# The thirteenth row of w_down in a staircase of small loads, ahead of the other twelve

## The chip, the cores and the metric

The kernel runs on one core of a Trainium2 chip. The metric is the device time of one execution in microseconds, as the median of several runs; lower is better. All engines of the core (TensorE, VectorE, ScalarE, GpSimd, SyncE) run their own instruction streams and meet at semaphores. Loads are issued by SyncE (SP in the profile) and carried out by the core's 16 DMA engines.

## The reference

One token goes through a decode step: attention over a cache of 4096 positions with 32 heads, then a gated feed-forward block, each behind a layer norm and with a residual.

```python
q = (x @ wq).reshape(B, Sq, Hq, Dh).transpose(0, 2, 1, 3)          # 640 -> 32 x 128
scores = jnp.einsum("bhqd,bhkd->bhqk", q, k) * (Dh ** -0.5)        # k_cache: 1 x 32 x 4096 x 128
o = jnp.einsum("bhqk,bhkd->bhqd", softmax(scores), v)
attn = o.transpose(0, 2, 1, 3).reshape(B, Sq, Hq * Dh) @ wo        # 4096 -> 640

g = jnp.einsum("bsd,df->bsf", x, w_gate)                           # 640 -> 1728
u = jnp.einsum("bsd,df->bsf", x, w_up)
ffn = jnp.einsum("bsf,fd->bsd", gelu(g) * u, w_down)               # 1728 -> 640

h = x + attn(layernorm(x), k_cache, v_cache, wq, wo)
out = h + ffn(layernorm(h), w_gate, w_up, w_down)
```

All tensors are bf16. The two caches are 32 MB each; with the weights 84 MB are read.

## The kernel before

The 32 heads are done in four groups of eight. For each group the K cache (8 MB) and the V cache (8 MB) are loaded as one transfer each into three large buffers `big`. VectorE multiplies K by the query (`mult`, L338), TensorE folds the products with an identity matrix (`fold`, L302 and L352), VectorE sums them to scores (`red`, L359), `soft` makes the exponentials (L388, L391), and `values` multiplies them with V on TensorE (L404). `Sched` keeps one list of instructions for each engine, in program order; a DMA increments its own semaphore by 16 when it has landed, and a waiting instruction names the count that it needs.

The order of the loads is the program order of SP's list. Behind the last V load come, in this order: `wo` (L445, it waits for the last fold), `w_gate` (L449), `w_up` (L449, it waits for `vfree[2]`, the end of the third group's `values`, since it lies in the buffer which that frees), and then `w_down` in `wd_sb`, which lies behind `w_up` in the same buffer.

`w_down` has 1728 rows of 640 elements. The first 1664 are laid out as 13 consecutive rows for each of the 128 partitions (`NM = 13`), so `wd_sb[:, b, :]` is the row b of every partition; the remaining 64 rows are a fourteenth column (`wd_sb[:, NM, :]`, on partitions 32 to 95), whose other partitions GpSimd fills with zeros first (L454). The loads are called wde (the 64 rows, L455) and wd0, wd1, wd2 (L460): the 13 rows are cut at `WD_CUTS = (0, 9, 12, 13)`, so these three carry 9, 3 and 1 rows for each of 128 partitions, in pieces of 11,520, 3,840 and 1,280 contiguous bytes.

The end of the kernel is a serial path: the output projection (L484), the second layer norm (L267 to L280), the two projections to 1728 (`up`, L502: first `w_gate`, then `w_up`), the transposes of their results to columns (L515), the gelu and the product `hm` (L522 to L531), the product with `w_down` (L537), two copies (L542, L543), one more (L545), and the store of 640 elements (L546). In L537 each of the 14 columns of `hm` is a stationary operand of four matmuls of 160 columns, one for each quarter of the output, on four strips of the array; a group waits for `hm` and for the load that holds its rows. The order of the groups is 13 first, then 0 to 12.

Of the kernel before, what the change touches and what calls it, by code (L numbers as in the profile page):

```python
# [35 lines left out]
NM = 13  # L36
NF = NM + 1
MF = NM * 128
E0 = 32
EP = DF - MF  # L40
WD_CUTS = (0, 9, 12, 13)
QF = NM * 32
NQ = D // 4

# [66 lines left out]
def bass_sequential_preLN__gqa_block_cached__glu_gated_geglu__decode_kernel(  # L111
# [12 lines left out]
    S = Sched(nc)  # L124
# [4 lines left out]
    def at(name, base, off, shape, dt=BF16):  # L129
        return nc.alloc_sbuf_tensor_at(name, shape, dt, offset=nc.lookup_mloc(base).addr + off)  # L130
# [6 lines left out]
    wd_sb = at("wd_sb", big[0], 2 * NC_D * DF, [128, NF, D])  # L137
# [70 lines left out]
    def vec(fn, waits=()):  # L208
        return S.op("vector", fn, waits)
# [33 lines left out]
    kfree, vfree = [None] * NG, [None] * NG  # L243
# [204 lines left out]
    def load_w(name, dst, src, lo, hi, wait):  # L448
# [5 lines left out]
    t_zr = S.op("gpsimd", lambda g: g.memset(wd_sb[:, NM, :], 0.0), [vfree[2]])  # L454
    d_we = S.dma("sync", "wde", lambda s: s.dma_start(  # L455
        wd_sb[E0:E0 + EP, NM, :], B_w_down[MF:DF, :]), [t_zr])
    d_wd = []
    for i in range(len(WD_CUTS) - 1):
        lo, hi = WD_CUTS[i], WD_CUTS[i + 1]
        tok = S.dma("sync", "wd%d" % i, lambda s, lo=lo, hi=hi: s.dma_start(  # L460
            wd_sb[:, lo:hi, :],
            B_w_down[0:MF, :].rearrange("(p b) n -> p b n", b=NM)[:, lo:hi, :]), [vfree[2]])
        d_wd += [tok] * (hi - lo)
    d_wd += [d_we]

    t_clear = vec(lambda v: v.memset(pf[1][:, :].rearrange("p (u x) -> p u x", u=2)[:, :, 0:32 * NF].rearrange(
# [13 lines left out]
    b = None  # L480
    for c in range(QD):
        for j in range(4):
            last = c == QD - 1 and j == 3
            b = S.op("tensor", lambda t, c=c, j=j: t.matmul(  # L484
                pd[32 * j:32 * j + 1, 0:NQ], aP[:, c:c + 1], wo_sb[:, c, j * NQ:(j + 1) * NQ],
                start=False, stop=False, skip_group_check=True), [t_aP, d_wo], token=last)
# [43 lines left out]
    t_u = columns(tu, pu, t_u)  # L530
    t_hm = vec(lambda v: v.tensor_mul(hm[:, :], gu[:, :], u_t), [a, t_u])  # L531

    order = [NM] + list(range(NM))
    for i, s in enumerate(order):
        for j in range(4):
            last = i == len(order) - 1
            b = S.op("tensor", lambda t, s=s, j=j, last=last: t.matmul(  # L537
                pd[32 * j:32 * j + 1, 0:NQ], hm[:, s:s + 1], wd_sb[:, s, j * NQ:(j + 1) * NQ],
                start=False, stop=last, skip_group_check=True),
                [t_hm, d_wd[s]], token=(last and j == 3))  # L540

    t_a = S.op("scalar", lambda a: a.copy(o_sb[:, 2 * NQ:3 * NQ], pd[64:128, 0:NQ]), [b])  # L542
    t_v = vec(lambda v: v.tensor_copy(o_sb[:, 0:NQ], pd[0:64, 0:NQ]), [b])  # L543
# [35 lines left out]
```

## Time and profile before

| | |
|---|---|
| median of 3 runs | 202.84 us (202.81 to 202.94) |
| the profiled execution | 202.74 us, span of the profile 201.5 us |
| TensorE clock granted, mean | 0.82 |
| busy: TensorE, VectorE, ScalarE, GpSimd | 114.3, 120.1, 10.0, 3.5 us |
| DMA | 84.32 MB in 2250 packets, mean 419 GB/s |
| wo, w_gate, w_up: issue to landing | 19.9, 24.6, 26.4 us |
| wd0, wd1, wd2, wde: issue to landing | 28.8, 29.3, 28.0, 26.0 us |

The profile is one execution; its span runs from the first to the last instruction, and 1.2 us of the measured time lie around it. In its lines, SPq is SyncE issuing a DMA, PE a matmul, PEld a weight load of TensorE, and the number behind L is the line of the kernel. A time in brackets is how long the engine sat idle before the instruction and what ended that. The three numbers of a piece of the chain are its start, its length and what it was.

### The profile page before, as it was taken

What the parts mean: (1) busy time and instruction counts of PE and PEld (TensorE: products, weight loads), DVE (VectorE), ACT (ScalarE), POOL (GpSimd) and SP (SyncE); (2) the same over time, 40 slices, a digit from 0 to 9 for tenths busy, and PEclk for the clock granted to TensorE, in tenths of its full rate; (3) what the DMA queues carried; (4) which work ended last, traced back from release to release, by engine and by line L of the source; (5) the groups of instructions that cost most, each with busy time, mean ns of one, the idle gap of its engine ahead of it and who ended that gap; (6) DMA issues with size and microseconds to landing.
All of it is one profiled execution on the core that took longest, in us unless ns stands there. A gap on an engine that the chain in (4) does not pass through costs nothing.

```text
span 201.5 us, 1615 instructions
## 1 busy us (share of the span) xinstructions
PE 114.3 (57%) x850; PEld 24.5 (12%) x560; DVE 120.1 (60%) x91; ACT 10.0 (5%) x28; POOL 3.5 (2%) x21
## 2 busy tenths in 40 slices
PE   1007930098508276876367059966634995864384
PEld 1000100000000030020022000200000033334332
DVE  2000570999993659998440499999899755010232
ACT  3000010000010101000101000000100002010000
POOL 5000000000000000000000000000000001000000
PEclk9999995569966969999967658999996698585855
DMA  7999999999999999999999999999999999999992
GB/s 252 398 586 416 416 429 416 416 416 416 416 416 507 468 468 407 416 429 416 416 418 433 416 416 481 468 455 416 416 442 416 416 429 444 390 407 429 422 403 95
DMA packets 2250, 84.32 MB, mean 419 GB/s; under 512 B 258, under 2 KB 452, under 8 KB 580
## 3 DMA queue, kind: packets, MB, share of 16 engines
q1 hardware_dynamic: 2242, 84.23, 97.2%
q8 instruction: 5, 0.08, 0.2%
q14 instruction: 1, 0.01, 0.0%
q10 hardware_dynamic: 2, 0.00, 0.0%
HBM read 84.23 MB, written 0.00 MB: 418 GB/s over the span
## 4 chain that ended last, share of the span: by engine, by line
DMA 48%; DVE 34%; PE 14%; issue 2%; ACT 1%; SPq 0%; DVEq 0%
DMA big<-in_A_k_cache_dram 35%; DVE big L338 22%; DMA wu_sb<-in_B_w_up_dram 13%; PE pf L302 7%; DVE sc L359 5%; PE pv L404 4%; DVE P L391 2%; DVE xz L328 2%; DVE qm L324 1%; PE pf L502 1%; PE pf L537 1%; PE pf L352 1%; ACT ex L388 1%; DVE mx L381 0%; DVE tu L515 0%
## 5 line engine op out<-in xcount | busy, mean ns | idle before, releaser
L338 DVE TENSOR_TENSOR big<-big,qb 128x8192 bf16<-128x8192 bf16 x16 | 70.2, 4418 | 19.6 <-DMA big<-in_A_k_cache_dram 19.6
L302 PE MATMUL pf<-big,Ibf 128*128 128x512 bf16 x240 | 62.0, 417 | 0.0
L352 PE MATMUL pf<-big,Ibf 128*128 128x512 bf16 x16 | 6.9, 433 | 47.8 <-DVE big L338 24.3
L359 DVE TENSOR_REDUCE sc<-pf 128x64 f32<-128x1024 f32 x16 | 19.3, 1218 | 10.2 <-PE pf L302 10.2
L404 PE MATMUL pv<-big,P 128*32 128x512 bf16 x192 | 15.0, 482 | 3.2 <-DVE P L391 3.2
L352 PEld LDWEIGHTS pf<-big,Ibf 128*128 128x128 bf16 x16 | 1.6, 98 | 94.7 <-DVE sc L359 54.4
L324 DVE TENSOR_TENSOR qm<-pf,hmask 128x1024 f32<-128x1024 f32 x2 | 2.4, 1224 | 17.2 <-PE pf L302 17.2
L316 PE MATMUL pf<-wq_sb,xb 128*128 128x512 bf16 x5 | 2.5, 504 | 12.6 <-DMA wq_sb<-in_A_wq_dram 12.6
L391 DVE TENSOR_TENSOR P<-ex,hmask_bf 128x2048 bf16<-128x2048 bf16 x3 | 6.9, 2293 | 2.0 <-ACT ex L388 2.0
L328 DVE TENSOR_REDUCE xz<-qm 128x128 f32<-128x1024 f32 x4 | 7.5, 1880 | 0.1
L404 PE MATMUL pv<-big,Pl 128*32 128x512 bf16 x64 | 6.1, 560 | 2.4 <-DMA big<-in_A_v_cache_dram 2.4
L404 PEld LDWEIGHTS pv<-big,P 128*32 128x32 bf16 x192 | 5.8, 118 | 11.1 <-issue 5.1
L388 ACT ACTIVATE ex<-sc,nb 128x256 bf16<-128x256 f32 x4 | 2.0, 508 | 86.3 <-DVE mj L385 86.3
L443 DVE TENSOR_TENSOR aT<-pm,rz 128x32 bf16<-128x32 f32 x1 | 0.2, 192 | 9.8 <-PE pm L415 9.8
L484 PE MATMUL pf<-wo_sb,aP 128*1 128x160 bf16 x128 | 3.9, 312 | 3.1 <-DMA wo_sb<-in_A_wo_dram 3.1
L302 PE MATMUL pf<-wq_sb,xb 128*128 128x512 bf16 x15 | 5.4, 480 | 0.0
L399 PE MATMUL pm<-rsm,ones 128*128 128x8 f32 x8 | 1.4, 251 | 6.8 <-ACT rsm L395 6.8
L415 PEld LDWEIGHTS pm<-cred,xm 128*128 128x128 f32 x32 | 4.0, 191 | 8.9 <-issue 6.5
L487 DVE STREAM_TRANSPOSE th<-pf 128x160 f32<-128x160 f32 x1 | 0.3, 350 | 7.6 <-PE pf L484 7.6
L415 PE MATMUL pm<-cred,xm 128*128 128x8 f32 x32 | 4.0, 252 | 1.4 <-ACT xm L412 1.4
L484 PEld LDWEIGHTS pf<-wo_sb,aP 128*1 128x1 bf16 x128 | 3.7, 116 | 3.3 <-issue 3.3
L331 ACT CAST qb<-xz 128x128 bf16<-128x128 f32 x4 | 1.2, 298 | 54.9 <-DVE xz L328 54.9
(85 smaller groups left out, 54.1 us busy)
## 6 DMA issues: line engine op xcount, KB each, us to landing
wq_sb<-in_A_wq_dram SPq DMA_DIRECT2D x1, 5120.0 KB, 15.2
wo_sb<-in_A_wo_dram SPq DMA_DIRECT2D x1, 5120.0 KB, 19.9
wg_sb<-in_B_w_gate_dram SPq DMA_DIRECT2D x1, 2160.0 KB, 24.6
wu_sb<-in_B_w_up_dram SPq DMA_DIRECT2D x1, 2160.0 KB, 26.4
wd_sb<-in_B_w_down_dram SPq DMA_DIRECT2D x1, 1440.0 KB, 28.8
wd_sb<-in_B_w_down_dram SPq DMA_DIRECT2D x1, 480.0 KB, 29.3
wd_sb<-in_B_w_down_dram SPq DMA_DIRECT2D x1, 160.0 KB, 28.0
wd_sb<-in_B_w_down_dram SPq DMA_DIRECT2D x1, 80.0 KB, 26.0
```

The costliest lines, as they stand in the source:

```text
L302: return t.add_instruction(m)
L316: return t.matmul(dst, xb[:, c, :], src, start=(c == 0), stop=last)
L324: a = t_qt[0] = vec(lambda v, i=i: v.tensor_tensor(out=qm[:, :, :], in0=pq[g][i][:, :].rearrange("p (h d) -> p h d", d=DH), in1=hmask[:, : ...
L328: t_qf[0] = vec(lambda v: v.reduce_sum(xz[:, :], qm[:, :, :].rearrange("p h d -> p d h"), axis=AX.X), [a, t_qb[gg - 1] if gg else None])
L338: return vec(lambda v: v.tensor_tensor(out=kb[g][:, s * RM:(s + 1) * RM, :], in0=kb[g][:, s * RM:(s + 1) * RM, :], in1=qb[:, g, :].unsquee ...
L352: return t.matmul(dst, Ibf[:, :], src, start=True, stop=False)
L359: red_done[n] = vec(lambda v: v.reduce_sum(sc[:, s * RM:(s + 1) * RM], pf[n % 2][:, :].rearrange("p (r w) -> p r w", r=RM), axis=AX.X), [f ...
L388: t_ex = S.op("scalar", lambda a: a.activation(ex[:, :], sc[:, :], ACTF.Exp, bias=nb[:, g:g + 1], scale=SCALE, accum_out=rs[:, g:g + 1]), ...
L391: t_p[g] = vec(lambda v: v.tensor_tensor(out=P[g][:, :, :], in0=ex[:, :].unsqueeze(2).to_broadcast([128, R, HG]), in1=hmask_bf[:, :].unsqu ...
L404: t_pv[g] = S.op("tensor", lambda t, i=i, r=r, q=q: t.matmul(pv[g % 2][q:q + 32, :], P[g][:, r:r + VR, :], vb[g][:, r:r + VR, :], start=(i ...
L415: t_acc[g] = S.op("tensor", lambda t, r=r: t.matmul(po[:, g * HG:(g + 1) * HG], xm[:, r, :], cred[:, r * HG:(r + 1) * HG], start=(r == 0), ...
L484: b = S.op("tensor", lambda t, c=c, j=j: t.matmul(pd[32 * j:32 * j + 1, 0:NQ], aP[:, c:c + 1], wo_sb[:, c, j * NQ:(j + 1) * NQ], start=Fal ...
```

## The change

The thirteenth row of each partition (`b = 12`) is taken out of the last of the three loads and is now loaded first, in sixteen small loads: fifteen of 15, 14, 13 and so on down to 1 partitions, and one of 8 (120 + 8 = 128). Each moves one row of 1,280 bytes for each of its partitions. The small loads count on two semaphores, `wds0` for the five that begin below partition 64 and `wds1` for the others; `d_wa` is the count of the first when complete, `d_ws` that of the second. The other twelve rows come behind, as 8, 3 and 1 rows. In L537 the groups now run in the order 13, 12, 0 to 11, all wait for `d_wa` as well, and group 12 for `d_ws`.

```diff
-WD_CUTS = (0, 9, 12, 13)
+WD_CUTS = (0, 8, 11, 12)
+STEPS = tuple(range(15, 0, -1)) + (8,)
...
     d_we = S.dma("sync", "wde", lambda s: s.dma_start(
         wd_sb[E0:E0 + EP, NM, :], B_w_down[MF:DF, :]), [t_zr])
+    rows = B_w_down[0:MF, :].rearrange("(p b) n -> p b n", b=NM)
+    p0 = 0
+    for m in STEPS:
+        d_ws = S.dma("sync", "wds%d" % (p0 // 64), lambda s, p0=p0, m=m: s.dma_start(
+            wd_sb[p0:p0 + m, NM - 1:NM, :], rows[p0:p0 + m, NM - 1:NM, :]), [vfree[2]])
+        if p0 < 64 <= p0 + m:
+            d_wa = d_ws
+        p0 += m
     d_wd = []
     for i in range(len(WD_CUTS) - 1):
         lo, hi = WD_CUTS[i], WD_CUTS[i + 1]
         tok = S.dma("sync", "wd%d" % i, lambda s, lo=lo, hi=hi: s.dma_start(
-            wd_sb[:, lo:hi, :],
-            B_w_down[0:MF, :].rearrange("(p b) n -> p b n", b=NM)[:, lo:hi, :]), [vfree[2]])
+            wd_sb[:, lo:hi, :], rows[:, lo:hi, :]), [vfree[2]])
         d_wd += [tok] * (hi - lo)
+    d_wd += [d_ws]
     d_wd += [d_we]
...
-    order = [NM] + list(range(NM))
+    order = [NM, NM - 1] + list(range(NM - 1))
     for i, s in enumerate(order):
...
                 start=False, stop=last, skip_group_check=True),
-                [t_hm, d_wd[s]], token=(last and j == 3))
+                [t_hm, d_wd[s], d_wa], token=(last and j == 3))
```

## The prediction

> **What bounds the kernel now.** I read the chain of waits in order of time first, because it says what the end hangs on. Its last stretch:
>
> ```profile
> 167.58 26.45 DMA wu_sb<-in_B_w_up_dram
> 194.03 0.04 issue
> 194.07 1.44 PE pf L502 x12
> ...
> 196.43 0.66 DVE tu L515
> ...
> 197.18 0.19 DVE hm L531
> ...
> 197.42 2.19 PE pf L537 x44
> ```
>
> The end hangs on the landing of `w_up` at 194.03. From there a serial path runs (L502, the transpose L515, `hm` L531) and the product with `w_down` (L537) can begin at 197.42 at the earliest. `w_up` stands ahead of all `w_down` loads in SP's queue, so nothing up to 197.42 is touched by the change. What it can move is L537, which takes from 197.42 to about 199.6, and what follows moves along. The timeline of that stretch:
>
> ```profile
> 197.42 0.09 PEld L537 LDWEIGHTS pf<-wd_sb,hm 128*1 128x1 bf16 x4 [1.60 <-DVE hm L531]
> 197.42 2.17 PE L537 MATMUL pf<-wd_sb,hm 128*1 128x160 bf16 x56 [1.05 <-DVE hm L531]
> 197.68 1.62 PEld L537 LDWEIGHTS pf<-wd_sb,hm 128*1 128x1 bf16 x52 [0.17 <-DMA wd_sb<-in_B_w_down_dram]
> ```
>
> The first four matmuls (row 13) run at 197.42; the next wait for the 9-row load wd0. In the trace's semaphore records wd0 lands at 197.64, wd1 (3 rows) at 198.78, wd2 (1 row) at 199.17. The weight loads that wait for them start at 197.68, 198.83 and 199.21, each 0.04 behind its landing. TensorE, at 0.133 us for a group of four, would come to the last two at nearly the same moments: engine and transfers are level here. So I looked next at how the transfers drain, by windows (the last two columns are the DMA engines' share and GB/s):
>
> ```profile
> 196.00:197.00 1.00, 0.37 (x6) 0.00 (x0) 0.57 (x1) 0.00 (x0) 0.00 (x0) 0.50 0.92 373
> 197.00:197.50 0.50, 0.08 (x4) 0.08 (x4) 0.26 (x2) 0.00 (x0) 0.00 (x0) 0.50 0.62 241
> 197.50:198.00 0.50, 0.50 (x16) 0.33 (x18) 0.00 (x0) 0.00 (x0) 0.00 (x0) 0.50 0.42 169
> 198.00:198.50 0.50, 0.50 (x24) 0.50 (x20) 0.00 (x0) 0.00 (x0) 0.00 (x0) 0.50 0.29 108
> 198.50:199.00 0.50, 0.50 (x28) 0.38 (x20) 0.00 (x0) 0.00 (x0) 0.00 (x0) 0.50 0.07 26
> ```
>
> The 16 DMA engines do not end together. Linking the trace's packets end to start gives sixteen chains. Nine send their last word at 196.98 to 197.35, seven at 197.90, 197.95, 198.44, 198.49, 198.52, 198.72 and 198.82. Five of these seven each carried a 16 KB instruction packet and lost about 1.5 us by it, one an 8 KB packet, one began late. The landing is that of the latest engine, 1.8 us behind the first.
>
> Last I read the issues on SP:
>
> ```profile
> 167.58 0.33 SPq L449 DMA_DIRECT2D wu_sb<-in_B_w_up_dram  x1
> 168.27 0.57 SPq L455 DMA_DIRECT2D wd_sb<-in_B_w_down_dram  x1
> 168.88 0.58 SPq L460 DMA_DIRECT2D wd_sb<-in_B_w_down_dram  x1
> 169.50 1.60 SPq L460 DMA_DIRECT2D wd_sb<-in_B_w_down_dram  x1
> 171.15 0.43 SPq L460 DMA_DIRECT2D wd_sb<-in_B_w_down_dram  x1
> ```
>
> They end at 171.58, while the first `w_down` packet moves only at 191.68: twenty microseconds ahead.
>
> **The change part by part.** *Sixteen more issues on SP.* The nearest rows are 0.31 us (the one-row store of L546) and 0.58; the three remaining loads move back by 16 x 0.31 to 16 x 0.58 = 5 to 9.3 us, so wd0 is issued at 174 to 178. Its first packet is due at 191.9, so the backlog hides this; behind the loads SP holds only the store of the result at 200.31. The cover is gone at (191.9 - 1.0 - 168.9) / 16 = 1.38 us per issue (1.0 is from SP's first issue at 0.80 to its first packet at 1.81). The 1.60 row is beyond that and makes a rival below.
>
> *The bytes.* None are added. If a load of m partitions goes to m engines with one row each, engines 0 to 15 carry 16, 15, 14, 13, 12, 11, 10, 9, then 7 down to 0 rows of the thirteenth, where each carried 8. In the trace a 1,280-byte packet follows another at 52 ns and the closing 4-byte word takes 6, so a small load costs 58 ns on an engine: wde's last word is followed by wd0's first packet 6 ns later, with no gap between loads. wd0's packets shrink from 11,520 bytes (428 ns apart) to 10,240, by the slope to the 3,840-byte packets (146 ns) 381 ns: 8 x 0.047 = 0.376 us less. So wd0 lands at its former time on an engine, plus 0.058 n - 0.376 for n small rows: -0.38 at n = 0, +0.55 at n = 16. wd1 and the last load keep their old sizes and shift alike, since through the last one the same thirteen rows have moved.
>
> *The order on TensorE.* Row 12 is now used second, in the 0.26 us in which row 13 was followed by the wait. It needs the small loads, which land by 195.2 at the latest (wde's last word at 193.80, 16 x 0.058, 0.4 of receipt), two microseconds ahead of `hm`. The two added waits stand in TensorE's queue ahead of 197.42, where wde's own wait (handled at 194.25) already stood; queued behind them are only L537's matmuls. Their 0.05 us rows lie under the wait for `hm`. I put them at nothing; uncovered they cost 0.1. The product then runs through: the last group could start at 197.42 + 0.085 + 12 x 0.133 = 199.10 instead of 199.23, a gain of 0.13 and no more.
>
> *The sum.* The end moves by the larger of -0.13 (TensorE's own pace) and x, the shift of the last load's landing (at 199.17 it released the last group directly). Everything hangs on which engines are late. The trace does not number them. A favourable order (the latest four at number 11 or above) gives the full -0.13; one with the latest engine at number 0 gives +0.55. Over random orders of the sixteen lateness values, I work out as an estimate a median of +0.26, a middle half of +0.15 to +0.39, and a quarter beyond +0.4. The five engines with instruction packets were hit in falling order of their first packet in the trace (places 13, 12, 10, 5 and 0 of 0 to 15), so lateness does go with some fixed order of the engines; that order taken as the engine number gives +0.14, its reverse +0.33. I take a value near the favourable end, about -0.05, because engines at fixed places are late and a staircase can meet them; both ends stay in the range.
>
> The profiled execution took 202.74 for a span of 201.5, with 1.24 around it that stays; the median of the runs is 0.10 higher. So 202.74 - 0.05 + 0.10 gives 202.8.
>
> **The rivals.** *The staircase is the wrong way round.* A late engine with a low number gets 9 to 16 rows: up to 202.84 + 0.55 = 203.4. For it: all engines have one speed here, and lateness comes from instruction packets that need not hit high numbers. Nine of the sixteen numbers (n of 7 and more) are worse off than before; x passes 0.4 from n = 14 on the latest engine.
>
> *SP's queue pushes back (slower).* Up to 23 loads are outstanding where the trace shows eight at most, and the seventh issue took 1.60. That issue ended at 171.10, just when the last engine closed the V cache load (171.09), which looks like a full queue. Against it: the next issue took 0.43 with as many small loads still out, so a count of loads is not what was full; weight of the large rows is likelier, and the new loads are light. At 1.60 each, wd0 is issued at 194.5, begins at 195.5, ends at 198.55 and lands at 198.95 instead of 197.64: +1.3, 204.1. It decides from 1.38 per issue. A hard limit near seven loads would issue wd0 at about 198.3 and add 5.
>
> *A load of 15 partitions does not go to 15 engines.* The trace shows 128 and 64 rows on sixteen engines, one row on one. Were the largest power of two taken that divides m, engine 0 would carry 86 rows, 4.57 us, and the end would be 2.3 to 4.2 later: 205.1 to 207.0. [...]
>
> *Each small load costs its full latency on its engine.* The one-row store takes 1.14 us from issue to landing; sixteen in series on engine 0 would be 18 us and the end near 219. The 6 ns between wde and wd0 speak against it. [...]
>
> *Faster by over 0.4.* TensorE's pace forbids it unless `w_up` itself lands earlier, as when instruction packets fall on other engines.
>
> **How the numbers follow.** About 0.2%, 0.4 us, is what a measurement of this kernel can tell from no change. The forecast (-0.13 to 0, 202.7 to 202.84) has 0.36; the wrong-way staircase 0.34, of which 0.22 stays under 0.4 and 0.12 goes beyond; the queue 0.14; the split 0.06; small-load latency 0.03; faster 0.07. That is 0.36 + 0.22 = 0.58 for the same, 0.12 + 0.14 + 0.06 + 0.03 = 0.35 for slower, 0.07 for faster. The range runs from 202.65 to 204.1: it holds the forecast, the staircase and the queue at 1.60, and leaves out about 0.2.
>
> **What would show it.** In the profile after: L537's weight loads without the wait of 0.17 before row 0; its 56 matmuls in about 2.0 instead of 2.17; sixteen issues of 0.3 to 0.6 on SP, ended by 180; the DMA share falling more steeply after 197 if the staircase meets the late engines, more slowly if not. I am wrong if wd0's issue stands behind 190, if TensorE waits for `w_down` for over 0.5, or if the landing of `w_up` moves from 194.0.

## The result and the profile after

The changed kernel took 203.95 us (203.57 to 204.14, six runs) beside 202.82 (202.78 to 202.94) for the kernel before: ratio 1.0053, 95% interval 1.004 to 1.0066. It is slower by 1.1 us. The forecast of 202.8 was wrong; the time lies within the range given with it. The profiled execution took 203.97, with a span of 202.7 instead of 201.5.

The end of the chain of waits no longer goes through `w_up` and `hm`; it goes through a load of `w_down`:

```profile
174.57 0.36 SPq L469
174.97 25.11 DMA wd_sb<-in_B_w_down_dram
200.13 0.73 PE pf L546 x12
200.88 0.33 DVE o_sb L552
```

The product with `w_down` has become L546. Its lines in the timeline:

```profile
197.47 0.10 PEld L546 LDWEIGHTS pf<-wd_sb,hm 128*1 128x1 bf16 x8 [1.37 <-DVE hm L540]
...
198.97 0.56 PEld L546 LDWEIGHTS pf<-wd_sb,hm 128*1 128x1 bf16 x32 [1.39 <-DMA wd_sb<-in_B_w_down_dram]
...
200.13 0.23 PEld L546 LDWEIGHTS pf<-wd_sb,hm 128*1 128x1 bf16 x12 [0.60 <-DMA wd_sb<-in_B_w_down_dram]
...
200.53 0.09 PEld L546 LDWEIGHTS pf<-wd_sb,hm 128*1 128x1 bf16 x4 [0.17 <-DMA wd_sb<-in_B_w_down_dram]
```

It starts where it did (197.47, 197.42 before) with two groups instead of one, since row 12 is there. Then it waits 1.39 us for wd0, 0.60 for wd1 and 0.17 for wd2. By the semaphore records wd0, wd1 and wd2 are complete at 198.93, 200.08 and 200.48, where they were at 197.64, 198.78 and 199.17: each 1.3 us later. The windows (last two columns: share of the DMA engines and GB/s) show the transfers that were to drain earlier draining later:

```profile
197.00:197.50 0.50, 0.03 (x4) 0.03 (x8) 0.32 (x2) 0.00 (x0) 0.00 (x0) 1.00 0.89 358
197.50:198.00 0.50, 0.28 (x8) 0.08 (x8) 0.00 (x0) 0.00 (x0) 0.00 (x0) 1.00 0.69 282
198.00:198.50 0.50, 0.00 (x0) 0.00 (x0) 0.00 (x0) 0.00 (x0) 0.00 (x0) 1.00 0.67 266
198.50:199.00 0.50, 0.03 (x4) 0.03 (x8) 0.00 (x0) 0.00 (x0) 0.00 (x0) 1.00 0.43 164
```

Before, these windows moved 241, 169, 108 and 26 GB/s. SP is not the cause. Its issues:

```profile
168.62 5.91 SPq L461 DMA_DIRECT2D wd_sb<-in_B_w_down_dram  x16
174.57 7.67 SPq L469 DMA_DIRECT2D wd_sb<-in_B_w_down_dram  x3
```

The sixteen new ones take 0.37 us each on average; wd0's issue stands at 174.57, and the last one takes 6.29 us and ends at 182.24. That is still 14 us ahead of what it moves.

The packet records show where the time is. In the kernel before, a packet takes nearly the same time for its size every time (17,280 bytes 644 to 651 ns, 11,520 bytes 432; 10,240 bytes mostly 385 in e1_one_load below), except where an instruction packet stands beside it. I call a packet stretched that takes over a tenth longer. Behind 185 us before has two stretched packets of these sizes, 1.0 us in sum; after has some 85 of all sizes, with 12.4 us in sum over the 16 engines. Eight of them, one beside an instruction packet, are packets of `w_up`, which stands ahead of everything the change touches: `w_up` is complete at 194.40 instead of 194.03. `hm` is late by only 0.06, because in this execution TensorE was granted 1.00 instead of 0.50 of its clock from 195.97 to 199.38. The weight load that waits for `w_up` and the line of `hm`, then two windows (the column before the last two is the granted clock):

```profile
194.44 0.11 PEld L511 LDWEIGHTS pf<-wu_sb,hln 128*1 128x1 bf16 x6 [0.71 <-DMA wu_sb<-in_B_w_up_dram]
...
197.24 0.18 DVE L540 TENSOR_TENSOR hm<-gu,tu 128x14 bf16<-128x14 f32 x1
```

```profile
195.00:196.00 1.00, 1.00 (x20) 0.45 (x8) 0.63 (x4) 0.21 (x1) 0.00 (x0) 0.52 0.89 337
196.00:196.50 0.50, 0.43 (x12) 0.09 (x2) 0.35 (x3) 0.00 (x0) 0.00 (x0) 1.00 0.91 338
```

Two of the three signs that the prediction had named for being wrong are here: TensorE waits for `w_down` for more than 0.5 us, and the landing of `w_up` has moved.

### The profile page after: what moved, and what is told of

The parts are those of the page before. It is cut to its first block, busy times and chain, and to the rows that moved or that the text cites. A ratio compares the mean times of both kernels' runs of the same rounds, so it can differ in the third digit from the quotient of the medians.

```text
span 202.7 us, 1631 instructions
## 1 busy us (share of the span) xinstructions
PE 115.3 (57%) x850; PEld 24.8 (12%) x560; DVE 120.1 (59%) x91; ACT 10.0 (5%) x28; POOL 3.5 (2%) x21
## 4 chain that ended last, share of the span: by engine, by line
DMA 47%; DVE 34%; PE 12%; SPq 3%; issue 2%; ACT 1%; POOL 0%; DVEq 0%
DMA big<-in_A_k_cache_dram 34%; DVE big L339 23%; DMA wd_sb<-in_B_w_down_dram 12%; PE pf L303 7%; DVE sc L360 5%; PE pv L405 4%; SPq L461 3%; DVE P L392 2%; DVE xz L329 2%; DVE qm L325 1%; PE pf L353 1%; ACT ex L389 1%; SPq L456 1%; DVE mx L382 0%; PE pf L546 0%
## 5 line engine op out<-in xcount | busy, mean ns | idle before, releaser
L317 PE MATMUL pf<-wq_sb,xb 128*128 128x512 bf16 x5 | 2.9, 573 | 12.8 <-DMA wq_sb<-in_A_wq_dram 12.8
L405 PE MATMUL pv<-big,Pl 128*32 128x512 bf16 x64 | 5.3, 507 | 3.0 <-DMA big<-in_A_v_cache_dram 3.0
L493 PE MATMUL pf<-wo_sb,aP 128*1 128x160 bf16 x128 | 4.4, 336 | 4.1 <-DMA wo_sb<-in_A_wo_dram 4.1
L303 PE MATMUL pf<-wq_sb,xb 128*128 128x512 bf16 x15 | 6.1, 535 | 0.0
L400 PEld LDWEIGHTS pm<-rsm,ones 128*128 128x128 f32 x8 | 1.7, 251 | 19.6 <-ACT rsm L396 16.2
```

Source lines behind the costliest of these rows:

```text
L303: return t.add_instruction(m)
L405: t_pv[g] = S.op("tensor", lambda t, i=i, r=r, q=q: t.matmul(pv[g % 2][q:q + 32, :], P[g][:, r:r + VR, :], vb[g][:, r:r + VR, :], start=(i ...
L493: b = S.op("tensor", lambda t, c=c, j=j: t.matmul(pd[32 * j:32 * j + 1, 0:NQ], aP[:, c:c + 1], wo_sb[:, c, j * NQ:(j + 1) * NQ], start=Fal ...
```

## The experiments

In the table, "over before" is the difference between the median and that of before on the same chip (202.69 for e1 to e4, 202.78 for e5 to e8, 202.72 for e9 to e12, 202.66 for e13 to e16, 202.71 for e17 and e18). The ratio is estimated by itself and need not equal the quotient of the medians. The columns behind it are read from the one profiled execution of each kernel: the landing of `w_up`, its stretched packets (one of them lies beside an instruction packet in every kernel), and the stretching of all packets behind 185 us in sum. For four kernels this execution is not typical: it took 203.41 in e5, 203.53 in e9, 202.90 in e11 and 203.39 in e13.

| kernel | us | over before | ratio, 95% | `w_up` at | stretched | sum, us |
|---|---|---|---|---|---|---|
| before | | | | 194.03 | 1 | 1.0 |
| after | 203.95 | 1.13 | 1.0053 (1.004, 1.0066) | 194.40 | 8 | 12.4 |
| e1_one_load | 202.76 | 0.07 | 1.0004 (0.9994, 1.0013) | 194.24 | 1 | 0.9 |
| e2_even16 | 203.63 | 0.94 | 1.0039 (1.0026, 1.0052) | 194.79 | 9 | 7.7 |
| e3_low8 | 205.15 | 2.46 | 1.0115 (1.0098, 1.0131) | 194.43 | 9 | 16.2 |
| e4_stairs_last | 204.44 | 1.75 | 1.008 (1.0065, 1.0095) | 193.99 | 1 | 2.6 |
| e5_two_of_64 | 203.9 | 1.12 | 1.0053 (1.0033, 1.0074) | 194.60 | 9 | 8.8 |
| e6_many_whole | 202.98 | 0.20 | 1.0008 (0.9998, 1.0017) | 194.14 | 1 | 1.3 |
| e7_even16_spread | 203.81 | 1.03 | 1.0047 (1.0032, 1.0062) | 194.49 | 11 | 10.1 |
| e8_low8_spread | 205.1 | 2.32 | 1.0093 (1.0062, 1.0124) | 194.41 | 5 | 16.3 |
| e9_own64 | 203.19 | 0.47 | 1.0024 (1.0014, 1.0035) | 194.17 | 2 | 1.3 |
| e10_foreign64 | 203.83 | 1.11 | 1.0053 (1.0037, 1.007) | 194.71 | 11 | 12.5 |
| e11_own8 | 203.37 | 0.65 | 1.0026 (1.0015, 1.0037) | 194.19 | 1 | 3.4 |
| e12_foreign8 | 204.02 | 1.30 | 1.0061 (1.0046, 1.0076) | 194.47 | 11 | 9.9 |
| e13_stairs_own | 203.79 | 1.13 | 1.0053 (1.0038, 1.0068) | 193.92 | 1 | 8.1 |
| e14_stairs_plain | 204.32 | 1.66 | 1.008 (1.0065, 1.0095) | 194.37 | 11 | 12.1 |
| e15_even16_own | 203.45 | 0.79 | 1.0039 (1.0024, 1.0054) | 194.02 | 1 | 4.1 |
| e16_even16_plain | 203.89 | 1.23 | 1.0057 (1.004, 1.0074) | 194.69 | 10 | 9.6 |
| e17_even32_own | 203.75 | 1.04 | 1.0048 (1.0031, 1.0064) | 194.54 | 10 | 9.2 |
| e18_half_rows_own | 204.78 | 2.07 | 1.0105 (1.009, 1.012) | 193.95 | 1 | 25.2 |

### What part of the change costs: e1 to e4

The first three keep all of the change but the sizes of the small loads; the fourth puts the sixteen loads behind wd0 to wd2 and row 12's group last.

```diff
-STEPS = tuple(range(15, 0, -1)) + (8,)
+STEPS = (128,)        # e1_one_load
+STEPS = (16,) * 8     # e2_even16
+STEPS = (8,) * 16     # e3_low8
```

> Row 12 comes ahead as one load of 128 partitions; cuts 8, 3, 1 and the order 13, 12, 0 to 11 as in the change. Theory A (the staircase puts rows on engines that are late: 0.4 to 0.5 us, and its foreign partitions slow other packets: 0.8 us): with no staircase the landing of wd0 goes back to 197.6 and the time to 202.7, that is 0.1 below before, and no 10,240-byte packet takes over 400 ns. Theory C (the new cuts or the order cost the time, whatever the shape of the small loads): 203.9 as with the change.

> [...] Theory A1 (only the number of rows on the late engines counts): wd0 lands within 0.05 us of the single load, 202.7 to 202.8, and packets of 10,240 bytes keep 385 ns. Theory A2 (rows written to other engines' partitions slow the large packets): packets of 440 to 860 ns as in the change and a time of 203.3 to 203.7.

> Row 12 in sixteen loads of 8 partitions: engines 0 to 7 carry 16 rows, 8 to 15 none. Theory A1: if the latest engines are among 8 to 15, wd0 lands 0.38 us earlier than with one load and TensorE sets the end, 202.7; if the latest is among 0 to 7 it lands 0.55 later, 203.4. Theory A2: on top of either, up to 0.8 us from slowed packets, 203.5 to 204.2.

```diff
     for i in range(len(WD_CUTS) - 1):      # e4_stairs_last: moved up
...
     for m in STEPS:                        # behind it
...
-    order = [NM, NM - 1] + list(range(NM - 1))
+    order = [NM] + list(range(NM))
-                [t_hm, d_wd[s], d_wa], token=(last and j == 3))
+                [t_hm, d_wd[s], d_wa if s == NM - 1 else None], token=(last and j == 3))
```

> The staircase comes behind the three other loads, and group 12 is last again. Theory A1 (rows on late engines alone): the last landing is that of the change without the slowed packets, 0.4 to 0.5 us later than before, 203.3. Theory A2: hardly any large packet is left beside the staircase, so most of the 0.8 us is gone: 203.2 to 203.4, and the 10,240-byte packets keep 385 ns. If the large packets are slow here too, the staircase is not what slows them, and the time stays at 203.9.

e1_one_load ends where before does: row 12 ahead, the cuts of 8, 3 and 1 and the new order on TensorE cost nothing and gain nothing. So the shape of the small loads is the whole of the 1.1 us. e2_even16 gives each engine eight rows as before, in eight loads of one row, and costs 0.94 with `w_up` itself 0.76 late: what costs is not only which engine has more rows. e3_low8 puts sixteen rows on eight of the engines and costs 2.46, where the prediction's 58 ns a row would make 0.55 at most. e4_stairs_last has no more stretched packets of the two large sizes than before (2.6 us in sum with the small ones), and yet TensorE waits last for the small loads:

```profile
200.77 0.09 PEld L546 LDWEIGHTS pf<-wd_sb,hm 128*1 128x1 bf16 x4 [1.30 <-DMA wd_sb<-in_B_w_down_dram]
```

wd2 was complete at 199.34. The last semaphore increments of the small loads came at 200.171, 200.356, 200.541 and 200.727: steps of 0.185 us, although an engine's packets for such a load take 58 ns in the records. The runs from e13 on come back to this.

### Few loads, many loads, other partitions: e5 to e8

```diff
-STEPS = tuple(range(15, 0, -1)) + (8,)
+STEPS = (64, 64)                              # e5_two_of_64
-WD_CUTS = (0, 8, 11, 12)
+WD_CUTS = tuple(range(9)) + (11, 12)          # e6_many_whole: nine loads of 1 row, then 3 and 1,
+STEPS = (128,)                                #   each for all 128 partitions
+    for i, p0 in enumerate(range(8)):         # e7_even16_spread
+        ps = slice(p0, p0 + 121, 8)
+    for i, p0 in enumerate(q + r for q in (0, 32, 64, 96) for r in range(4)):   # e8_low8_spread
+        ps = slice(p0, p0 + 29, 4)
```

> Row 12 in two loads of 64 partitions: 4 rows for each of 16 engines in each, 8 in all, and only two closing words for each engine. [...] Theory S (each small load costs an engine some 70 ns through its closing word): two words more are 0.14 us, hidden, 202.7 and no slow packets. [...]

> Many loads, each of all 128 partitions: row 12 ahead, then rows 0 to 7 as eight loads of one row, then 3 and 1. Twelve loads of w_down with twelve closing words for each engine where the change has up to sixteen, and eight rows of 1,280 bytes for each engine in a load. From the packets of the kernel before (52 ns for 1,280 bytes, 381 for 10,240) this costs 8 x 8 x 52 - 8 x 381 = 0.28 us of transfer. [...] Theory S: eight words more at 70 ns add 0.56 on every engine, 203.3 to 203.6, and packets behind them are stretched.

> As the eight loads of 16 partitions (0.8 us over before), but each takes every eighth partition instead of sixteen neighbours: same engines, same rows, same closing words, other partitions. [...] Theory S: nothing changes, 203.6.

> [...] Theory S: sixteen closing words as before, 205.1.

e5_two_of_64 was a miss: two loads cost as much as sixteen. The four runs of e5 lie between 203.41 and 204.45, so its size is rough. e6_many_whole has seven more loads than e1_one_load, all of 128 partitions, and is at most 0.17% slower than before: this many whole loads cost next to nothing. The spread kernels go with their counterparts (e7 with e2, 1.03 to 0.94; e8 with e3, 2.32 to 2.46), so it makes no difference that shows whether the rows of a load go to neighbouring partitions or to every eighth or fourth. From e6 I concluded that a price per load was out. That was too quick, since its loads have eight rows for each engine. A price per row is out by e6, in which each engine moves more than seventy rows in packets of their own.

### Where the rows land: e9 to e12

If the number and the size of the loads do not explain e5, the place might. Each pair loads the same rows in loads of the same shape as well, ahead of wd0, into unused memory; only the destination partitions differ. The packet records hold sizes and times but no partitions. So "own" and "foreign" in the labels, and theory G's talk of which engine fills which partitions in whole loads, are an assumption of mine that no run shows; what the pairs compare is partitions 32 to 95 twice with 0 to 63 and 64 to 127 (e9, e10), and every fourth of 0 to 63 with every fourth of 64 to 127 (e11, e12).

```diff
+    for i, p0 in enumerate((32, 32)):         # e9_own64;  (0, 64) in e10_foreign64
+        d_scr = S.dma("sync", "scr", lambda s, i=i, p0=p0: s.dma_start(
+            scr[p0:p0 + 64, i:i + 1, :], rows[64 * i:64 * i + 64, NM - 1:NM, :]), [vfree[2]])
...
+    for i, r in enumerate((0, 1, 2, 3, 32, 33, 34, 35)):    # e11_own8;  64 + r in e12_foreign8
+        d_scr = S.dma("sync", "scr", lambda s, r=r: s.dma_start(
+            scr[0 + r:0 + r + 29:4, 0:1, :], rows[r:r + 29:4, NM - 1:NM, :]), [vfree[2]])
```

> The kernel before with two further loads of 64 rows each (row 12 of w_down's partitions 0 to 63, then 64 to 127; 164 KB in all) issued between wde and wd0 into unused memory, both to partitions 32 to 95. [...] The output doesn't depend on them. Theory G (a row costs again where the engine that carries it is not the one that fills that group of partitions in whole loads): no 10,240 B packet longer than 450 ns but for those beside instruction packets, every landing of w_down later by eight rows at 52 to 58 ns = 0.42 to 0.46 us, time +0.3 to +0.5, so 203.1 to 203.3. Rival H (any load of fewer than 128 partitions stretches the packets beside it): the same as e10_foreign64, 203.9 to 204.4.

> [...] Theory G: stretched 10,240 B and 17,280 B packets of 6 to 9 us in sum, time 1.0 to 1.6 over before, 203.8 to 204.4, and 0.6 to 1.1 over e9_own64. Rival H: no difference between the two. Rival R (it is the source rows or the number of loads that cost, not where they land): no difference either.

> [...] Theory G: no stretching; the first eight engines carry eight rows more at 52 to 58 ns, 0.42 to 0.46 us, the last eight none; time +0.1 to +0.45, 202.9 to 203.25. Rival H: stretching as in e3_low8 for half as many rows, 7 to 8 us in sum, 203.6 to 204.4.

> [...] Theory G: stretched packets of 5 to 8 us in sum, time 203.6 to 204.4, and the last eight engines, which carry none of the small rows, run late as well by 0.4 us or more. Rivals H and R: the same time as e11_own8.

The pairs are 0.64 and 0.65 apart, and the intervals of their ratios do not meet: where a row lands has a price of its own. e9_own64 costs just the transfer of its rows, 0.47 for an expected 0.42 to 0.46. The mark is in `w_up`: in e10 and e12 eleven of its packets are stretched, in e11 only the one beside an instruction packet. e11_own8 missed its figure: 0.65 instead of at most 0.45. Its ten runs go from 202.64 to 203.56, and the profiled one, at 202.90, is among the three fastest; it has fifteen stretched packets of wd0 beside the one by an instruction packet. So the distance between the two profiles below is larger than that between the medians. TensorE's waits in e11 and e12:

```profile
197.83 1.63 PEld L542 LDWEIGHTS pf<-wd_sb,hm 128*1 128x1 bf16 x52 [0.17 <-DMA wd_sb<-in_B_w_down_dram]
```

```profile
198.97 1.65 PEld L542 LDWEIGHTS pf<-wd_sb,hm 128*1 128x1 bf16 x52 [1.02 <-DMA wd_sb<-in_B_w_down_dram]
```

### The same for the change's own shape: e13 to e16

```diff
+    for j, m in enumerate(tuple(range(15, 0, -1)) + (8,)):     # e13, e14;  (16,) * 8 in e15, e16
+        q0 = 32 + j % 4
+        d_scr = S.dma("sync", "scr", lambda s, j=j, m=m, p0=p0, q0=q0: s.dma_start(
+            scr[q0:q0 + 4 * m - 3:4, j // 4:j // 4 + 1, :],    # e14, e16: scr[p0:p0 + m, 0:1, :]
+            rows[p0:p0 + m, NM - 1:NM, :]), [vfree[2]])
+        p0 += m
```

> [...] Nothing is taken out of wd0 to wd2, so eight rows of transfer, 0.42 to 0.46 us, come on top of what the change costs. Theory G (landing in another engine's group is what costs): the large packets keep their 432 ns, an engine with n rows is 0.058 n later, time +0.4 to +0.9, 203.2 to 203.7. Rival U (loads that leave the engines unequal cost by themselves): as e14_stairs_plain, 204.1 or more.

> As e13_stairs_own with the same loads, rows and engines, but landing in consecutive partitions as in the change. Both theories: the change's 1.1 us and 0.42 us for the added rows, 204.1 to 204.6. Theory G: 0.6 us or more over e13_stairs_own; rival U: no more than 0.2 over it.

> [...] Theory G: no stretching but for single packets beside instruction packets, time +0.42 to +0.5, 203.15 to 203.3. If many single rows cost by themselves (rival M): two stretched packets or so to each engine as in e11_own8, 32 of them, and 203.5 or more. Theory U: as G here, since the engines stay equal.

> As e15_even16_own, landing in consecutive partitions as in e2_even16. Theory G: e2_even16's 0.9 us and 0.42 for the added rows, 203.9 to 204.3, with 35 or more stretched 11,520 B packets. Rival M: no more than 0.2 over e15_even16_own.

Landing on partitions 0 to 127 in order instead of on 32 to 95 costs 0.53 in the staircase and 0.44 in the even shape, less than expected; the intervals of each pair overlap, so these two sizes are rough. But again it is visible in `w_up` (11 and 10 stretched packets instead of 1) and through it in `hm`. In e15_even16_own and e16_even16_plain:

```profile
197.17 0.18 DVE L539 TENSOR_TENSOR hm<-gu,tu 128x14 bf16<-128x14 f32 x1
```

```profile
197.84 0.18 DVE L538 TENSOR_TENSOR hm<-gu,tu 128x14 bf16<-128x14 f32 x1
```

The other half is a second cost. e13_stairs_own lies 0.23 above its upper bound, and e15_even16_own, eight rows to each engine and all on partitions 32 to 95, is 0.32 slower than e9_own64 with the same bytes and the same partitions in two loads. The intervals of e9 and e15 overlap, so these times alone do not show it. But e13 and e15 have long packets of wd0 (25 and 19, on sixteen engines; e9 has two), and of `w_up` only the one beside an instruction packet.

The profile of e13_stairs_own shows where this cost begins. Linked end to start, the packets form sixteen chains with 0 to 7 and 9 to 16 small rows, each number once, as one row of a load to each of m engines gives. On each I take the time from the closing word of `w_up` to that of wd0, less the 3.65 us that it takes before:

| small loads on the engine | 4 | 5 | 6 | 7 | 9 | 10 | 12 | 14 | 16 |
|---|---|---|---|---|---|---|---|---|---|
| packets alone, at 58 ns, us | 0.23 | 0.29 | 0.35 | 0.41 | 0.52 | 0.58 | 0.70 | 0.81 | 0.93 |
| measured, us | 0.23 | 0.29 | 0.35 | 0.48 | 1.22 | 1.31 | 1.55 | 1.72 | 2.13 |

Up to six loads in a row cost their packets and no more. From nine on there is 0.7 us and more on top, in stretched packets of wd0, although all rows lie on partitions 32 to 95, as in e9_own64.

### Does the second cost go by the number of loads: e17 and e18

```diff
+    for j in range(4):                        # e17_even32_own: four loads of 32 rows
+            scr[q0:q0 + 63:2, col:col + 1, :], rows[32 * j:32 * j + 32, NM - 1:NM, :]), [vfree[2]])
...
+    for j in range(16):                       # e18_half_rows_own: sixteen loads of 16 half rows
+            scr[q0:q0 + 61:4, j // 4:j // 4 + 1, 0:D // 2],
+            rows[p0:p0 + 16, NM - 1:NM, D // 2 * (j % 2):D // 2 * (j % 2) + D // 2]), [vfree[2]])
```

> [...] If the second cost goes by the number of loads behind each other (theory N): half of e15's 0.33 us over the bytes' 0.46, time 0.55 to 0.68 over before, fewer than 19 stretched 11,520 B packets. If it goes by the rows (rival W) or is a fixed price of loads of one row: as e15, 0.75 to 0.85, or as e9, 0.47, with 15 or more stretched packets or none.

> As e15_even16_own with sixteen loads of 16 half rows (640 B) instead of eight of 16 rows: the same bytes on each engine, twice the loads. Theory N: the bytes' 0.46 and the added closing words' 0.05, and 0.5 to 0.7 of stretching, time 1.0 to 1.2 over before, with 30 or more stretched 11,520 B packets. Rival W: as e15, 0.75 to 0.95 over before, with 20 or so.

e18_half_rows_own settles it: the bytes of e15 in twice the loads cost 2.07 instead of 0.79, more than expected. It has twice the packets as well, but the number of packets is not what costs: e6 has more of them on each engine, in loads of all 128 partitions, without the stretching. `w_up` and `hm` (197.10) are on time; wd0 is 2 us late:

```profile
199.65 0.74 PEld L544 LDWEIGHTS pf<-wd_sb,hm 128*1 128x1 bf16 x36 [2.22 <-DMA wd_sb<-in_B_w_down_dram]
```

Its small packets follow each other at 28 ns with 6 for the closing word, so all sixteen are through in 0.55 us on an engine. The semaphore increments come in steps of about 0.17 us (196.472, 196.652, 196.826, 197.000), 2.7 us for sixteen, and on every engine the first packet of wd0 takes 1.27 to 1.68 us instead of 0.43. So on an engine one load closes every 0.17 to 0.20 us, whether it has 1,280 bytes there (0.197 in e15) or 640 (0.174 in e18). As I read it, the packets run ahead of that for a while, and then a large one behind them is held up: the first of wd0 in e18, mostly the third or fourth in e15. Packets and stretching together delay an engine by 2.1 us on average in e18 (0.55 and 1.54), and sixteen loads of whole rows delayed theirs by 2.13 in e13: the price goes by the loads, not by their bytes. The lead is, as an estimate, 0.7 us from e18 (16 x (0.174 - 0.034) = 2.2 less 1.5), 0.9 from e15 (8 x (0.197 - 0.058) = 1.1 less 0.2) and 0.4 to 0.7 from e13 (nine and sixteen loads at its steps of 0.179, less the 1.22 and 2.13 of the table). One rival was not tested: the small loads of a kernel count on one or two semaphores together, while each whole load of e6 has its own.

e17_even32_own does not answer its question. It has all marks of e10 and e12 (ten stretched packets of `w_up`, which lands at 194.54), although its rows lie on partitions 32 to 95 like those of e9 and e15. So the partitions alone do not settle the price of the place. Of its 1.04, 0.46 would be the bytes; why the other 0.58 come here, no run shows.

## Why the prediction was wrong

**The step that failed is "the bytes": "a small load costs 58 ns on an engine".** 58 ns is the time of its packets, and by e13 it holds for up to six such loads in a row, but not for the nine to sixteen that half of the engines carry. Landings are further apart than that: in the kernel after, the last semaphore increments of the small loads come at 196.057, 196.253, 196.449 and 196.645, steps of 0.196. I had read the 6 ns between wde's last word and wd0's first packet as "no gap between loads"; it is a distance of packets. The last closing word of the small loads is moved at 194.63, and their last increment comes at 196.65. For the place where a row lands the step had no term at all.

How the 1.31 us of wd2's landing come about, for the latest engine (ten small rows, by linking packets end to start; the sixteen chains again have 0 to 7 and 9 to 16 small rows, each number once): the prediction's own term gives 0.058 x 10 - 0.376 = +0.20. Its wd0 packets are stretched by 0.81 us; as an estimate from the steps, 10 x (0.196 - 0.058) = 1.4, less the 0.4 to 0.9 of lead, 0.5 to 1.0. Its last two packets of `w_up` took 793 and 791 ns instead of 644, which is 0.30. Together 1.31, set against the latest engine of the kernel before, as if the two were equally late otherwise. In times, e14 less before, 1.66, less the 0.42 of added rows, makes 1.24 beside the 1.13 of the change; roughly 0.53 of it is the place (e14 less e13), and the other 0.7 is the staircase with the steps of its increments.

Why a load closes in steps of 0.17 to 0.20 us, no run shows. Nor does one show why the place has a price: I laid out e9 to e16 by an assumption on which engine fills which partitions, and no trace here names a partition. What they show is the price: 0.64 and 0.65 in e9 to e12, 0.53 and 0.44 in e13 to e16.

**"Nothing up to 197.42 is touched by the change"** failed too. The small loads are issued behind `w_up`, but the engines are apart: in the kernel after, the increments of `w_up` run from 192.18 to 194.40, and the first of the small loads' landings comes at 192.59. So early engines moved small rows while late ones were still on `w_up`; that the rows' place is what slowed these is my reading of the pairs. Linked end to start, the stretched packets of `w_up` in the kernel after, but for the one beside an instruction packet, are the last one or two of the six latest engines; the ten that were through with `w_up` by 192.2 have none. It lands at 194.40 instead of 194.03, and in e2_even16 and e10_foreign64, with no such rise of the clock, `hm` is 0.76 and 0.68 late.

**"The small loads land by 195.2 at the latest"**: they landed at 196.65. Even so row 12 was there before `hm`.

**"Sixteen more issues" and "the order"** held. The issues took 5.9 us where 5 to 9.3 were given, e1_one_load shows the order at nothing, and the two groups ahead of the wait ran as described. The gain of 0.13 was never to be seen, since the transfers became the bound.

**The rivals.** *The staircase the wrong way round* holds in direction, with +0.20 of its bound of 0.55. *SP's queue*: one issue did take 6.29 us, and that stays hidden. *The split*, which no run had shown either way, did not happen: the two semaphores of the small loads show 65 and 63 increments at landings, one for each row, and the chains have 0 to 7 and 9 to 16 small packets, one row to each of m engines. *Full latency on each engine* had a chance of 0.03 at 219 us. Its mechanism, loads in series on an engine, came nearest; its price of 1.14 was six times too high, and "the 6 ns between wde and wd0 speak against it" was the misreading above. **"A value near the favourable end"** of the lateness was a guess without a row behind it, and the estimate's median of +0.26 would have been the better one.

## What to carry to other kernels

Don't cut a load into pieces of a few rows where the DMA engines are the bound, even if its packets seem to add up: each piece closes on its engine in its own 0.17 to 0.20 us here, and nine or more pieces shorter than that in a run made the load behind them late (up to six did not, in e13). Nine loads of all 128 partitions with 0.42 us of packets on each engine cost nothing that is clear of the noise (e6_many_whole). A load of fewer partitions can slow a load that was issued before it (`w_up` at 194.71 in e10_foreign64 instead of 194.03). To price a small load from a trace, read the distances between its semaphore increments, not those between its packets.

## What was not expected of the hardware

A load issued behind another one delayed it: `w_up`'s packets of 17,280 bytes took up to 1.00 us instead of 0.64 (e12). Two loads of 64 partitions cost 1.12 us (e5_two_of_64), although every engine has the same bytes as with one of 128 (0.07); the place made only 0.64 between e9 and e10, so the size of this one stays open. So does what sets the lead of 0.4 to 0.9 us that packets have over their increments, and why the cost sets in between six and nine loads. Row 12 of a partition has to lie on that partition, so this staircase cannot land all its rows on partitions 32 to 95; another order of its loads was not tried. Of all kernels run, none was faster than the one before.
